# Reordering the first up-projections, and the scores and masks of chunk 1, in a fused attention and feed-forward kernel

## The chip, the cores and the metric

The kernel runs on one NeuronCore of a Trainium2 chip. The metric is device time in microseconds (us), the median of several executions; lower is better. Each comparison alternates runs of a kernel with runs of the kernel before on one chip.

## The reference

Sliding-window causal attention (8 batches, 8 heads, 576 positions, head size 64, window 64), then a feed-forward layer with a quick GELU over the 4608 tokens.

```python
scores = scale * np.matmul(q, k.transpose(0, 1, 3, 2))
mask = (rel >= 0) & (rel < window)            # rel = query position - key position
attn = softmax(np.where(mask, scores, -1e9))  # written out in the reference
attn_out = np.matmul(attn, v)
x = attn_out.transpose(0, 2, 1, 3).reshape(B * S, H * D)      # 4608 x 512
h = x @ w_in                                   # 512 -> 2048
g = h * (1.0 / (1.0 + np.exp(-1.702 * h)))
out = g @ w_out                                # 2048 -> 512
```

## The kernel before

Tokens are handled in 36 blocks of 128, attention by block (`scores`, `exp`, `mask`, `pv` for the value products, `norm`, then a transpose `x_mm` on TensorE and its copy `x_out`), the feed-forward by chunks of four blocks: 16 up-projections (`up`), each of a matmul part, a tanh on ScalarE and a gate on VectorE, then `down`. The program order is written by hand, and the trace shows an instruction that is ready wait for the one ahead of it: a mask whose exp had ended at 66.39 us started at 68.00, behind a gate. The matmuls write to tiles in PSUM from three pools: psH and psO with two buffers each, psT with one.

```python
def up_mm(ch, f, nf, t0, nt, wide=False):
    pool, tag = (psO, "O") if wide and next(turns) % 2 else (psH, "H")   # 2 buffers each
    ps = pool.tile([P, nf, nt], fp32, name="hps", tag=tag)
    ...                                   # nf x 4 matmuls
def up_th(ps, ...):  # ScalarE: th = tanh(0.851 * ps)
def up_g(th, ps, ...):  # VectorE: gT = (th + 1) * ps
def up(*args, **kw):
    up_g(*up_th(*up_mm(*args, **kw)))
```

The start: weights are loaded by GpSimd between its casts of values.

```python
for i in range(2):
    cast_v(0, i)
nc.gpsimd.tensor_copy(out=gate[0:1, 0:1], in_=stage_qk[1][0:1, 1, 0:1])
load_w_in(0)
cast_v(0, 2)
load_w_in(1)
cast_v(0, 3)
load_w_in(2)
load_w_in(3)
...
scores(3)
mask(2)
exp(3)
...
warm(6)                                   # six idle matmuls
pv(2)
norm(2)
u = up_mm(0, 0, 4, 0, P, wide=True)
mask(3)
x_mm(2, psO, "O")
x_out(2)
u = up_th(*u)
pv(3)
norm(3)
up_g(*u)
up(0, 0, 4, P, P, wide=True)
up(0, 0, 4, 2 * P, P, wide=True)
x_mm(3, psT, "T")
x_out(3)
up(0, 0, 4, 3 * P, P, wide=True)
for f in range(4, 16):
    up(0, f, 1, 0, 512, wide=True)
```

Chunk 1, in which attention of blocks 5 to 9 is woven between the up-projections of blocks 4 to 7:

```python
for m in range(4, 8):
    t0 = (m % 4) * P
    ...
    u = up_mm(1, 0, 4, t0, P, wide=True)
    pv(m + 1)
    up_g(*up_th(*u))
    norm(m + 1)
    up(1, 4, 4, t0, P, wide=True)
    ...                                   # m = 4, 6: turn_pairs, casts
    up(1, 8, 4, t0, P, wide=True)
    ...                                   # casts, loads, transposes for batch 2
    scores(m + 2)
    exp(m + 2)
    x_mm(m + 1, psT, "T")
    x_out(m + 1)
    up(1, 12, 4, t0, P, wide=True)
    mask(m + 2)
```

From chunk 2 on the order is by slots; from chunk 4 on x is transposed by DMA.

The softmax here doesn't subtract the row's maximum and nothing guards it: scores larger than these inputs give would overflow.

## Time and profile before

| | |
|---|---|
| timed at first | 323.79 us median of 3 (323.31 to 323.87) |
| profiled run | 328.4 us, span 326.7 us, mean clock 0.984 |
| TensorE busy | 94% of the span |
| VectorE, ScalarE, GpSimd busy | 51%, 48%, 42% |

The page's groups read: line, engine, operation, out<-in, shapes, count | busy us, mean ns of one | idle us of the engine just before them and what ended most of it. These two groups have the longest waits on VectorE and ScalarE:

```profile
L371 DVE SCALAR_TENSOR_TENSOR gT<-th,hps 128x512 bf16<-128x512 bf16 x144 | 99.0, 688 | 118.1 <-ACT th L365 118.0
L365 ACT ACTIVATE th<-hps 128x512 bf16<-128x512 f32 x144 | 86.1, 598 | 118.2 <-PE hps L354 109.3
```

The gates of VectorE wait for tanh, tanh waits for TensorE. Little of this idle time reached TensorE, which was busy for 94% of the span: it waited 3.2 us for masks (2.3 and 0.9 in the two groups of value products, L296). What cost time was an instruction queued behind such a waiting gate that could have run already and whose result TensorE wanted: for the mask at 68.00 us TensorE waited 0.78 us.

### The profile page before, as it was taken

What the parts mean: (1) busy time and instruction counts of PE and PEld (TensorE: products, weight loads), DVE (VectorE), ACT (ScalarE), POOL (GpSimd) and SP (SyncE); (2) the same over time, 40 slices, a digit from 0 to 9 for tenths busy, and PEclk for the clock granted to TensorE, in tenths of its full rate; (3) what the DMA queues carried; (4) which work ended last, traced back from release to release, by engine and by line L of the source; (5) the groups of instructions that cost most, each with busy time, mean ns of one, the idle gap of its engine ahead of it and who ended that gap; (6) DMA issues with size and microseconds to landing.
All of it is one profiled execution on the core that took longest, in us unless ns stands there. A gap on an engine that the chain in (4) does not pass through costs nothing.

```text
span 326.7 us, 7994 instructions
## 1 busy us (share of the span) xinstructions
PE 306.4 (94%) x3320; PEld 200.7 (61%) x3320; DVE 165.6 (51%) x284; ACT 157.5 (48%) x249; POOL 136.8 (42%) x197
## 2 busy tenths in 40 slices
PE   7888997777899899999999999999999999999995
PEld 7675453676777577777777777775555554444442
DVE  5666525556755536555556556555555554443300
ACT  2666416365555536545445455555545444344411
POOL 1880427856997677666776357700000000000000
PEclk9799999799999979999999999999999999999999
DMA  8999899999999999999999999934333311100021
GB/s 190 202 178 214 209 253 239 224 157 175 118 108 117 134 159 125 180 143 134 169 167 163 176 168 153 121 82 107 89 81 83 93 53 48 34 32 33 32 98 64
DMA packets 151524, 43.32 MB, mean 133 GB/s; under 512 B 135104, under 2 KB 146368, under 8 KB 151488
## 3 DMA queue, kind: packets, MB, share of 16 engines
q0 software_dynamic: 73008, 13.05, 60.1%
q1 hardware_dynamic: 74448, 22.43, 39.2%
q10 hardware_dynamic: 4032, 7.34, 6.5%
q8 instruction: 26, 0.43, 0.6%
q14 instruction: 10, 0.08, 0.1%
HBM read 36.70 MB, written 9.44 MB: 141 GB/s over the span
## 4 chain that ended last, share of the span: by engine, by line
PE 84%; DVE 5%; ACT 5%; DMA 3%; issue 1%; POOL 0%; POOLq 0%; ACTq 0%
PE ops L384 38%; PE hps L354 36%; PE Tacc L296 4%; PE S L267 3%; DMA kt<-rows_k 3%; ACT th L365 2%; PE idle L405 2%; DVE gT L371 1%; DVE PT L282 1%; ACT E L277 1%; PE turn L149 1%; ACT xT_pe L335 1%; PE pxt L330 1%; DVE qt L104 1%; DVE xs L309 1%
## 5 line engine op out<-in xcount | busy, mean ns | idle before, releaser
L371 DVE SCALAR_TENSOR_TENSOR gT<-th,hps 128x512 bf16<-128x512 bf16 x144 | 99.0, 688 | 118.1 <-ACT th L365 118.0
L384 PE MATMUL ops<-w_out_sb,gT 128*128 128x512 bf16 x576 | 144.4, 381 | 0.5 <-DVE gT L371 0.5
L365 ACT ACTIVATE th<-hps 128x512 bf16<-128x512 f32 x144 | 86.1, 598 | 118.2 <-PE hps L354 109.3
L354 PEld LDWEIGHTS <-w_in_sb 128*128 128x128 bf16 x1328 | 108.2, 114 | 43.8 <-issue 4.7
L384 PEld LDWEIGHTS <-gT 128*128 128x128 bf16 x576 | 53.2, 98 | 52.2 <-issue 1.1
L354 PE MATMUL hps<-xT_dma,w_in_sb 128*128 128x256 bf16 (+1 forms) x448 | 82.5, 318 | 0.0
L354 PE MATMUL hps<-xT_pe,w_in_sb 128*128 128x128 bf16 (+1 forms) x880 | 67.1, 232 | 3.5 <-ACT xT_pe L335 3.5
L277 ACT ACTIVATE E<-S 128x1024 bf16<-128x1024 f32 x36 | 36.7, 1020 | 3.6 <-PE S L267 3.6
L188 POOL DMA_DIRECT2D v_nat<-in_v_dram x25 | 21.3, 852 | 21.4 <-issue 12.4
L398 ACT ACTIVATE o_sb<-ops 128x512 f32<-128x512 f32 x34 | 20.4, 600 | 19.0 <-PE ops L384 18.7
L309 DVE TENSOR_TENSOR xs<-Tacc,rc 128x512 bf16<-128x512 f32 x36 | 24.9, 692 | 1.2
L282 DVE TENSOR_TENSOR PT<-E,mask_None 128x1024 bf16<-128x1024 bf16 x28 | 20.6, 737 | 1.7 <-ACT E L277 1.7
L192 POOL COPY v_off<-v_nat 64x528 bf16<-64x528 bf16 x25 | 15.6, 630 | 13.8 <-DMA v_nat<-in_v_dram 13.0
L187 POOL DMA_DIRECT2D rows_k<-in_k_dram x25 | 21.4, 854 | 0.0
L187 POOL DMA_DIRECT2D rows_q<-in_q_dram x25 | 21.1, 846 | 0.0
L267 PE MATMUL S<-qt,kt 64*128 64x64 bf16 x576 | 16.1, 191 | 5.0 <-DMA kt<-rows_k 1.6
L267 PEld LDWEIGHTS <-kt 64*128 64x128 bf16 x576 | 11.1, 95 | 12.9 <-issue 6.2
L296 PE MATMUL Tacc<-v_off,PT 128*64 128x65 bf16 x320 | 16.4, 200 | 0.9 <-DVE PT L282 0.9
L92 POOL CAST v_off<-stage_v 64x512 bf16<-64x512 f32 x15 | 9.4, 630 | 17.5 <-DMA stage_v<-in_v_dram 16.6
L296 PE MATMUL Tacc<-v_nat,PT 128*64 128x65 bf16 x256 | 14.6, 200 | 2.3 <-DVE PT L282 2.3
L296 PEld LDWEIGHTS <-PT 128*64 128x64 bf16 x576 | 12.4, 112 | 6.4 <-DVE PT L282 4.2
L194 POOL COPY v_off<-v_nat 64x528 bf16<-64x528 bf16 x20 | 13.2, 659 | 1.2
(47 smaller groups left out, 127.7 us busy)
## 6 DMA issues: line engine op xcount, KB each, us to landing
out_dram<-o_sb ACTq DMA_DIRECT2D x28, 256.0 KB, 3.2
stage_v<-in_v_dram SPq DMA_DIRECT2D x12, 256.0 KB, 6.5
rows_q<-in_q_dram POOLq DMA_DIRECT2D x20, 128.0 KB, 5.5
rows_k<-in_k_dram POOLq DMA_DIRECT2D x20, 128.0 KB, 5.9
v_nat<-in_v_dram POOLq DMA_DIRECT2D x20, 128.0 KB, 5.7
stage_qk<-in_q_dram SPq DMA_DIRECT2D x4, 512.0 KB, 5.4
stage_qk<-in_k_dram SPq DMA_DIRECT2D x4, 512.0 KB, 6.0
w_in_sb<-in_moe_w_in_dram POOLq DMA_DIRECT2D x4, 512.0 KB, 5.9
```

The costliest lines, as they stand in the source:

```text
L187: nc.gpsimd.dma_start(out=heads(rows[b % 2][w][0:n, i, :]), in_=rows_of(src, b, i))
L188: nc.gpsimd.dma_start(out=v_nat[b % 2][0:n, i, :, 0:D], in_=rows_of(v, b, i))
L267: nc.tensor.matmul(st[:, h % 2, t * 256 + hp * 64 : t * 256 + hp * 64 + 64], lhsT=src[1][part, hp, 64 * j : 64 * j + 128], rhs=src[0][part ...
L277: nc.scalar.activation(out=E_of[m][:], in_=S_of.pop(m)[:], func=AF.Exp, scale=scale)
L282: nc.vector.tensor_tensor(out=pt[:].rearrange("p a f -> p (a f)"), in0=E_of.pop(m)[:].rearrange("p a f -> p (a f)"), in1=masks[z][:].rearr ...
L296: nc.tensor.matmul(acc[t * 64 : t * 64 + 64, h // 4, (h % 4) * 66 : (h % 4) * 66 + 65], lhsT=pt[:, epos : epos + 64], rhs=win, start=True, ...
L309: nc.vector.tensor_tensor(out=xs[:].rearrange("p (b h d) -> p b h d", b=2, h=4), in0=view[:, :, :, 0:D], in1=rc[:].to_broadcast([P, 2, 4, D]),
L354: nc.tensor.matmul(ps[:, g, :], lhsT=w_in[:, c, (f + g) % 4 : 512 : 4], rhs=xT[ch][:, m0 : m0 + nt // P, c, :], start=(c == 0), stop=(c == 3),
L365: nc.scalar.activation(out=th[:], in_=ps[:], func=AF.Tanh, scale=0.851)
L371: nc.vector.scalar_tensor_tensor(out=gT[ch, f // 4][:, f % 4 : f % 4 + nf, t0 : t0 + nt], in0=th[:], scalar=1.0, in1=ps[:], op0=ALU.add, o ...
L384: nc.tensor.matmul(O_of[ch, tsub][:, :], lhsT=gT[ch, j][:, f, tsub * P : (tsub + 1) * P], rhs=w_out_sb[:, 4 * j + f, :], start=(j == 0 and ...
L398: nc.scalar.activation(out=o_sb[:], in_=ps[:], func=AF.Copy, scale=0.5)
```

## The change

Its intent: in chunk 0, to give TensorE up-projections to do while it waits for masks, normalising and x copies; in chunk 1, to run each mask while VectorE idles for the last tanh, and in blocks 5 and 7 to let exp start earlier by moving the scores up by one unit.

```diff
-    warm(6)
+    warm(4)
+    u0 = up_mm(0, 0, 4, 0, P, wide=True)
     pv(2)
     norm(2)
-    u = up_mm(0, 0, 4, 0, P, wide=True)
+    u1 = up_mm(0, 0, 4, P, P, wide=True)
+    u0 = up_th(*u0)
     mask(3)
     x_mm(2, psO, "O")
+    u1 = up_th(*u1)
     x_out(2)
-    u = up_th(*u)
+    up_g(*u0)
     pv(3)
     norm(3)
-    up_g(*u)
-    up(0, 0, 4, P, P, wide=True)
+    up_g(*u1)
     up(0, 0, 4, 2 * P, P, wide=True)
+    up(0, 4, 4, 0, P, wide=True)
     x_mm(3, psT, "T")
     x_out(3)
+    up(0, 4, 4, P, P, wide=True)
+    up(0, 4, 4, 2 * P, P, wide=True)
     up(0, 0, 4, 3 * P, P, wide=True)
-    for f in range(4, 16):
+    up(0, 4, 4, 3 * P, P, wide=True)
+    for f in range(8, 16):
         up(0, f, 1, 0, 512, wide=True)
...
     (chunk 1; the moved turn_pairs and casts are cut)
-        up(1, 8, 4, t0, P, wide=True)
...
+        if m in (4, 6):
+            up(1, 8, 4, t0, P, wide=True)
         scores(m + 2)
         exp(m + 2)
+        if m in (5, 7):
+            u = up_mm(1, 8, 4, t0, P, wide=True)
+            mask(m + 2)
+            up_g(*up_th(*u))
         x_mm(m + 1, psT, "T")
         x_out(m + 1)
-        up(1, 12, 4, t0, P, wide=True)
-        mask(m + 2)
+        u = up_mm(1, 12, 4, t0, P, wide=True)
+        if m in (4, 6):
+            mask(m + 2)
+        up_g(*up_th(*u))
```

More of the change, by code (lines that the diff above doesn't have):

```diff
@@ L536 @@
         up(1, 4, 4, t0, P, wide=True)
+        if m in (4, 6):
+            turn_pairs(1, m // 2 - 1, turn_tiles(psT, "T"))
         if m == 4:
-            turn_pairs(1, 1, turn_tiles(psT, "T"))
             cast_v(1, 2)
@@ L543 @@
             cast_v(1, 4)
-        if m == 6:
-            turn_pairs(1, 2, turn_tiles(psT, "T"))
-        up(1, 8, 4, t0, P, wide=True)
-        if m > 4:
+        else:
             cast_qk(2, m - 5)
@@ L555 @@
         load_v(2, m - 3)
+        if m in (4, 6):
+            up(1, 8, 4, t0, P, wide=True)
         scores(m + 2)
         exp(m + 2)
+        if m in (5, 7):
+            u = up_mm(1, 8, 4, t0, P, wide=True)
+            mask(m + 2)
+            up_g(*up_th(*u))
         x_mm(m + 1, psT, "T")
         x_out(m + 1)
-        up(1, 12, 4, t0, P, wide=True)
-        mask(m + 2)
+        u = up_mm(1, 12, 4, t0, P, wide=True)
+        if m in (4, 6):
+            mask(m + 2)
+        up_g(*up_th(*u))
     pe = {}
```

## The prediction

> **What bounds the kernel now.** I read the page first (busy shares, slices, chain), then the waits between engines, then each engine's timeline in 16 to 40 us (chunk 0) and 56 to 122 us (chunk 1 and the start of chunk 2), then DMA landings. Page of the kernel before:
>
> ```profile
> span 326.7 us, 7994 instructions
> PE 306.4 (94%) x3320; PEld 200.7 (61%) x3320; DVE 165.6 (51%) x284; ACT 157.5 (48%) x249; POOL 136.8 (42%) x197
> ...
> PE   7888997777899899999999999999999999999995
> ...
> PEclk9799999799999979999999999999999999999999
> ```
>
> TensorE is the bound: no other engine is over 51%, and from slice 16 on (8.17 us each) it is full. Only its gaps in slices 0 to 14 can be won. The clock row has three dips (slices 1, 7, 14). In 0.1 us windows, the clock is half from 12.99 to 16.37, 57.35 to 60.77 and 115.37 to 118.79 us. After about 125 us the waits view has no TensorE wait worth naming, so time won earlier should reach the end.
>
> The gaps of chunk 1, TensorE timeline (start, duration, operation, idle before and its releaser):
>
> ```profile
> 66.92 1.05 PE L354 MATMUL hps<-xT_pe,w_in_sb 128*128 128x128 bf16 x16 [0.44 <-ACT xT_pe L335]
> 68.75 0.22 PE L296 MATMUL Tacc<-v_nat,PT 128*64 128x65 bf16 x1 [0.78 <-DVE PT L282]
> ...
> 69.12 1.98 PE L354 MATMUL hps<-xT_pe,w_in_sb 128*128 128x128 bf16 x32
> 71.03 0.41 PE L267 MATMUL S<-qt,kt 64*128 64x64 bf16 x16
> 71.38 0.40 PE L330 MATMUL pxt<-ident,xs 128*128 128x128 bf16 x4
> 71.61 1.06 PE L354 MATMUL hps<-xT_pe,w_in_sb 128*128 128x128 bf16 x16
> 73.18 1.05 PE L354 MATMUL hps<-xT_pe,w_in_sb 128*128 128x128 bf16 x16 [0.52 <-ACT xT_pe L335]
> ```
>
> One block (up-projection 0, value products, up-projections 4 and 8, scores, x transposes, up-projection 12) takes 73.18 - 66.92 = 6.26 us, twice waiting: value products for a mask, the next block's first up-projection for the x copy. Why these come late, ScalarE and VectorE timelines:
>
> ```profile
> 65.36 1.03 ACT L277 ACTIVATE E<-S 128x1024 bf16<-128x1024 f32 x1
> 66.28 0.59 ACT L335 COPY xT_pe<-pxt 128x512 bf16<-128x512 bf16 x1
> 66.75 0.62 ACT L365 ACTIVATE th<-hps 128x512 bf16<-128x512 f32 x1
> ```
>
> ```profile
> 67.40 0.69 DVE L371 SCALAR_TENSOR_TENSOR gT<-th,hps 128x512 bf16<-128x512 bf16 x1 [1.21 <-ACT th L365]
> 68.00 0.68 DVE L282 TENSOR_TENSOR PT<-E,mask_None 128x1024 bf16<-128x1024 bf16 x1
> ```
>
> The exp ended at 66.39, yet its mask starts at 68.00, behind a gate that waited 1.21 us for a tanh. The x copy stands behind the exp, which starts only after the scores.
>
> [...] each dip is 3.4 us[...]. [...] the last dip follows one wait of 1.62 us. [...] In the trace, key transposes landed in 2.4 us (issued 65.98) to 8.2 us (issued 105.98), the latter beside GpSimd's loads[...].
>
> **The change, part by part.** Durations: an up-projection of 16 128x128 matmuls is 0.89 us on the chain, of four 128x512 0.865; its tanh starts 1.15 us after its start, tanh 0.60, gate 0.69, exp 1.02, mask 0.68, x copy 0.58, value products 0.38, scores 0.34, x transposes 0.24; normalising ends 1.48 after the value products start (68.75 to 70.23). Queued ScalarE and VectorE work starts some 0.09 us before its predecessor ends.
>
> *Chunk 0.* It removes two warm matmuls, fills the mask wait with real work, and splits four 512-wide up-projections into four 128-wide ones: 8x0.89 + 8x0.865 for 4x0.89 + 12x0.865, +0.1 us. Before, scores end at 18.93 and the last up-projection at about 36.6; the removable gaps there are 0.28, 0.20 and 0.94 plus two warms. After, step by step: the first up-projection waits for its weights (issued 13.54, landing 5.9 later, 19.44): 19.5 to 20.39. Value products 2 to 20.77, second up-projection to 21.66, x transposes 2 wait for normalising, 21.94. Mask 3 follows it on VectorE, to 22.46; value products 3 at 22.52 to 22.9. The x copy queues behind the second tanh, to 23.0; third up-projection 23.06 to 23.95. The fourth needs the PSUM buffer of the second, two psO allocations back, whose gate now queues behind normalising 3, to 24.6: 24.65 to 25.54, a **new wait** of 0.7. Then all is ready: x transposes 0.24, four 128-wide, eight 512-wide: 25.54 + 0.24 + 3.56 + 6.92 = 36.26. **Gain 0.35 us**, of 1.6 that one might hope for.
>
> *Chunk 1, masks ahead of gates.* The mask moves from 68.00 to 66.42, while VectorE idles for the gate's tanh. Value products start right after the up-projection, at 67.8 instead of 68.75: 0.95 for that block.
>
> *Chunk 1, scores one unit up* (blocks 5 and 7). Value products 67.81 to 68.19, up-projection 4 to 69.08, scores to 69.42; exp behind tanh 4, 69.8 to 70.82; up-projection 8 to 70.31; x transposes to 70.53, up-projection 12 to 71.42. Tanh 8 is 70.72 to 71.32, x copy 71.21 to 71.80: next block at 71.86, for 73.18. That is 4.94 us a block for 6.26, **1.32 each, 2.64 for two**, mask gain included. TensorE work alone is 4.45, so some 0.45 stays idle before each next block.
>
> *Block 6* (73.18 to 80.90, 7.72 us). Value products gain again, but transposes of pairs need the psT buffer that normalising frees, and normalising sits behind the first gate: they start 3.37 after the block's start, for 3.43 before. The rest gains where key copies no longer find VectorE behind a late gate: the next block at 78.92, 7.06 us, **gain 0.66**. Block 4 gains nothing before its end.
>
> Sum: 0.35 + 2.64 + 0.66 = **3.65 us**; chunk 2 starts at 83.5 instead of 87.16.
>
> *What lies after.* TensorE runs dense to 112.4, where scores of block 13 wait for keys:
>
> ```profile
> 114.27 0.29 PE L267 MATMUL S<-qt,kt 64*128 64x64 bf16 x8 [1.62 <-DMA kt<-rows_k]
> 114.87 1.44 PE L384 MATMUL ops<-w_out_sb,gT 128*128 128x512 bf16 x4
> ```
>
> Their transpose is issued behind an output store that follows TensorE, so both come 3.65 earlier and the lead stays. What changes is the neighbours: GpSimd's loads run ahead by their own clock. The issue moves to 102.3; the windows view shows a DMA share of 0.60 in 102 to 106, for 2.03 in 106 to 112.4. The wait may shrink, and with it the dip (estimate 1.8: pieces of 1.37, 1.71, 0.43 and 1.09 us on the chain for 0.86, 0.89, 0.22 and 0.86). Together up to 3.4 more.
>
> **Rivals.** (1) *The key wait goes too:* 3.65 + 3.4 = 7.05, 316.7 us. For it: the quieter DMA stretch. Against: loads issued from 103.35 still overlap, and the profiled run took 328.4 us for 323.79 unprofiled, so part of that wait may exist only under the profiler. (2) *The gain runs into DMA:* TensorE is 3.65 us nearer to its data and the same wait lengthens, leaving 1.5 to 2 us of gain, 322. For it: the view of waits has GpSimd waiting 8.0 us for loads in 60 to 125. Against: keys of batch 2 were issued by 83 with 3 to 6 us to land, long before use. (3) *ScalarE takes over in chunk 1*, delaying the x copies: gain under 2, 322. Against: 3.4 us of work in a block of 4.94. (4) [...] each dip is worth about 1.8 us either way; moving 0.35 us should keep the one at 57.
>
> **Range and chances.** The middle: 323.79 - 3.65 = 320.1; a third of rival 1's extra 3.4, less 0.2 for slips, gives 319.2. Low 316.6 is rival 1; high 321.6 is 2.2 us of gain, rival 2 or 3 in part. Over 2% needs 317.3, which asks for most of rival 1: 0.18. Slower by 2% would need several new waits: 0.01.
>
> **What would show it.** Right: no mask wait before value products of blocks 6 and 8; two blocks of about 4.9 us; a psO wait of about 0.7 before the fourth up-projection of chunk 0, whose end moves only some 0.35; chunk 2 beginning about 83.5. Wrong: blocks still over 5.5 us, an x copy later than ScalarE's order says, a longer key wait near 109 us, or another count of dips.

## The result

The changed kernel took 321.99 us (median of 4, 321.62 to 322.43), the kernel before 323.56 us (median of 4) beside it: ratio 0.9951, 95% interval 0.9934 to 0.9969. A ratio here is the mean time of one kernel's fast runs over that of the other's of the same rounds, so it is not quite the ratio of the medians. The gain was 1.6 us where the prediction's middle asked for 4.6, and the time lies 0.4 us above the stated range. All outputs are right.

The experiments repeated the comparison three times, the second and third on one chip, the fourth on another; the chip of the first is not on record:

| comparison | changed, median us | before, median us | ratio, 95% interval |
|---|---|---|---|
| first | 321.99 (4 runs) | 323.56 (4) | 0.9951, 0.9934 to 0.9969 |
| second | 321.19 (6) | 324.15 (11) | 0.9900, 0.9864 to 0.9936 |
| third | 321.51 (6) | 324.28 (12) | 0.9928, 0.9886 to 0.9969 |
| fourth | 321.65 (6) | 325.15 (11) | 0.9896, 0.9867 to 0.9924 |

The second and third share eleven runs of the kernel before, so they are not independent. The changed kernel's medians stayed within 321.2 to 322.0 us. The kernel before was lowest in the first comparison, the one the prediction is held against. By the later three the gain is 2.6 to 3.3 us (differences of means); all four are gains of under 2%.

Page of the changed kernel, first profile (clock in tenths of full speed, 40 slices):

```profile
span 320.7 us, 8047 instructions
...
PE   7869997798999999999999999999999999999994
...
PEclk9999999879999999999999999999999999999999
```

The spans of the two first profiles differ by 6.0 us, nearly four times the timed gain, and the trace says what the 6.0 is made of. The first down-projection began at 35.33 for 36.59 (1.26): the kernel before had half clock from 12.99 to 16.37 in its profile (granted clock 0.50; such a stretch of half clock is called a dip here), the changed one had not. Chunk 1 took 28.89 for 30.19 us (1.30), with two dips for one. From the start of chunk 2 to the end it took 236.1 for 239.5 (3.4): the wait for keys and the dip behind it were gone. So 4.7 of the 6.0 lie in dips and a wait that later profiles show to come and go. In chunk 1 it is the other way round: without dips the changed kernel takes 26.63 us there (runs 2, 4 and 5), so two dips, at 55.8 and at 66.0, hid 2.3 us of the gain in this execution, which is one of the four that were timed.

Block 7 of chunk 1 in the changed kernel, at full clock. TensorE's timeline (start, duration, what, count, idle before and releaser), then VectorE's:

```profile
79.57 1.05 PE L354 MATMUL hps<-xT_pe,w_in_sb 128*128 128x128 bf16 x16 [0.44 <-ACT xT_pe L335]
...
80.93 1.08 PE L354 MATMUL hps<-xT_pe,w_in_sb 128*128 128x128 bf16 x16
81.94 0.41 PE L267 MATMUL S<-qt,kt 64*128 64x64 bf16 x16
82.28 1.08 PE L354 MATMUL hps<-xT_pe,w_in_sb 128*128 128x128 bf16 x16
83.20 0.39 PE L330 MATMUL pxt<-ident,xs 128*128 128x128 bf16 x4
83.43 2.21 PE L354 MATMUL hps<-xT_pe,w_in_sb 128*128 128x128 bf16 x32
```

```profile
79.07 0.78 DVE L282 TENSOR_TENSOR PT<-E,mask_None 128x1024 bf16<-128x1024 bf16 x1 [0.23 <-ACT E L277]
80.05 0.69 DVE L371 SCALAR_TENSOR_TENSOR gT<-th,hps 128x512 bf16<-128x512 bf16 x1 [0.20 <-ACT th L365]
```

The mask now runs ahead of the gate, and the value products (the lines left out after the first) no longer wait. The last line holds two units, the second of chunk 2: it starts 2.21 - 1.05 = 1.16 us after 83.43, at 84.59. The block took 84.59 - 79.57 = 5.02 us, for 6.26 before; 4.94 was predicted.

Chunk 0 is another picture:

```profile
19.20 1.09 PE L354 MATMUL hps<-xT_pe,w_in_sb 128*128 128x128 bf16 x16 [1.65 <-DMA w_in_sb<-in_moe_w_in_dram]
20.59 1.08 PE L354 MATMUL hps<-xT_pe,w_in_sb 128*128 128x128 bf16 x16
...
22.84 1.95 PE L354 MATMUL hps<-xT_pe,w_in_sb 128*128 128x128 bf16 x32
...
35.33 1.03 PE L384 MATMUL ops<-w_out_sb,gT 128*128 128x512 bf16 x3
```

The first up-projection waited 1.65 us for its weights, with the value products of block 2 behind it. The third and fourth are one group of 1.95 us, twice 0.89 and a tail of some 0.16, so the fourth began at 22.84 + 0.89 = 23.73: the psO wait of 0.7 us that was predicted ahead of it is not there. VectorE's timeline has the gate of the second unit, for which it was to wait:

```profile
23.68 0.68 DVE L371 SCALAR_TENSOR_TENSOR gT<-th,hps 128x512 bf16<-128x512 bf16 x1
```

The gate was as late as predicted (it ended at 24.36, for 24.6), and the fourth up-projection started while that gate was still reading its tile. So the two did not share a buffer.

### The profile page after: what moved, and what is told of

It reads as the page before. It is cut to its first block, busy times and chain, and to the rows that moved or that the text cites. A ratio compares the mean times of both kernels' runs of the same rounds, so it can differ in the third digit from the quotient of the medians.

```text
span 320.7 us, 8047 instructions
## 1 busy us (share of the span) xinstructions
PE 299.2 (93%) x3329; PEld 200.6 (63%) x3366; DVE 164.7 (51%) x284; ACT 157.4 (49%) x249; POOL 135.3 (42%) x197
## 4 chain that ended last, share of the span: by engine, by line
PE 83%; ACT 5%; DMA 4%; DVE 3%; issue 3%; SPq 2%; POOL 0%; ACTq 0%
PE ops L384 38%; PE hps L354 37%; PE Tacc L296 4%; PE S L267 3%; DMA stage_qk<-in_k_dram 2%; DMA w_in_sb<-in_moe_w_in_dram 2%; ACT th L365 2%; ACT E L277 1%; ACT xT_pe L335 1%; PE turn L149 1%; DVE gT L371 1%; SPq L85 1%; SPq L119 1%; PE pxt L330 1%; DVE xs L309 1%
## 5 line engine op out<-in xcount | busy, mean ns | idle before, releaser
L384 PE MATMUL ops<-w_out_sb,gT 128*128 128x512 bf16 x539 | 136.6, 379 | 5.3 <-issue 4.1
L354 PEld LDWEIGHTS <-w_in_sb 128*128 128x128 bf16 x1376 | 110.5, 115 | 42.0 <-issue 2.3
L354 PE MATMUL hps<-xT_pe,w_in_sb 128*128 128x128 bf16 (+1 forms) x928 | 68.2, 230 | 3.5 <-DMA w_in_sb<-in_moe_w_in_dram 1.6
```

What stands on the lines that cost most here:

```text
L354: nc.tensor.matmul(ps[:, g, :], lhsT=w_in[:, c, (f + g) % 4 : 512 : 4], rhs=xT[ch][:, m0 : m0 + nt // P, c, :], start=(c == 0), stop=(c == 3),
L384: nc.tensor.matmul(O_of[ch, tsub][:, :], lhsT=gT[ch, j][:, f, tsub * P : (tsub + 1) * P], rhs=w_out_sb[:, 4 * j + f, :], start=(j == 0 and ...
```

## Experiments

My theory after the result: (A) chunk 1 gains as predicted; chunk 0 is paced by the landing of the first weights, so its reorder gives nothing; and the profile of the kernel before was a slow draw. Rivals: (B) the wait for keys is a standing cost that the change takes away; (C) chunk 0's new order costs time and eats part of chunk 1's gain; (D) half-clock dips eat it; later (E) the gain runs into a new wait on DMA. The runs came in four groups: runs 1 to 4, 5 to 8 and 9 to 12 on one chip, 13 to 15 on another. Each group is compared with runs of the kernel before; those of the second group are the first group's eleven and one more.

**1. The kernel before, unchanged.** No edit.

> The kernel before, unchanged, for a second profile. Theory A (the profile on record was a slow draw: it took 328.4 us where timed runs took 323.3 to 323.9): the new profile is near 322 us of span, has no 1.6 us wait for keys at scores of block 13, and at most two half-clock dips (mean clock 0.989 or more). Rival B (the key wait is in every run and the change removed it): the wait of 1 us or more shows again. Ratio to the kernel before 1.000 either way.

Measured: 324.97 us, ratio 1.0014 (0.9978 to 1.0049); profiled run 325.69 us, span 323.9 where theory A had 322.

```profile
18.92 1.08 PE L354 MATMUL hps<-xT_pe,w_in_sb 128*128 128x128 bf16 x16 [0.71 <-DMA w_in_sb<-in_moe_w_in_dram]
...
113.17 0.29 PE L267 MATMUL S<-qt,kt 64*128 64x64 bf16 x8 [1.48 <-DMA kt<-rows_k]
```

Theory A is half right. There was one dip and not three, and the weights already hold up the old order, by 0.71 us after its value products. But the wait for keys is there: part of rival B holds. In the five profiles without the whole new chunk 1 it was 1.62 (first), 1.48, 0.82 (run 3), 0.8 (run 9, masks alone) and none (run 10, scores alone).

**2. The changed kernel, unchanged.** No edit.

> The changed kernel, unchanged, as the control for the two halves. Both theories: ratio 0.993 to 0.997, about 1.6 us under the kernel before. Its profile should again show blocks of about 4.95 us where the clock is full.

Measured: 321.19 us, ratio 0.9900 (0.9864 to 0.9936), a larger gain than at first and than expected; no wait for keys. In this profile the weights held chunk 0 up twice:

```profile
18.93 1.08 PE L354 MATMUL hps<-xT_pe,w_in_sb 128*128 128x128 bf16 x16 [1.19 <-DMA w_in_sb<-in_moe_w_in_dram]
...
25.33 1.08 PE L354 MATMUL hps<-xT_pe,w_in_sb 128*128 128x128 bf16 x16 [1.71 <-DMA w_in_sb<-in_moe_w_in_dram]
...
36.95 1.03 PE L384 MATMUL ops<-w_out_sb,gT 128*128 128x512 bf16 x3
```

The second wait is for the second quarter of the weights, which the new order uses one unit earlier and ahead of the x transposes of block 3. That load landed 8.2 us after its issue here and 5.5 in the first profile.

**3. Chunk 0 alone.** The first hunk of the diff on the kernel before.

> Only the reordering of chunk 0. Theory A (chunk 0 is paced by the landing of the first weights at about 19.2 us, and the new order does not shorten what follows): ratio 0.999 to 1.002. Prediction on record: 0.35 us, ratio 0.9989. Rival C (the new order of chunk 0 costs time, and eats part of chunk 1's gain): ratio 1.002 to 1.005, 0.6 to 1.6 us slower.

Measured: 324.64 us, ratio 1.0014 (0.9984 to 1.0044). The reorder of chunk 0 shows no gain; one of 0.35 us (0.9989) lies inside the interval, one of 0.6 does not. Its first up-projection began at 19.38 and the first down-projection at 35.50.

**4. Chunk 1 alone.** The second hunk on the kernel before.

> Only the reordering of chunk 1. Prediction on record: 3.3 us, ratio 0.990. Theory A (a half-clock dip that moves into or stays in chunk 1 hides part of it): ratio 0.993 to 0.996. Rival C (chunk 0's reorder loses what chunk 1 wins): ratio 0.988 to 0.991 here, clearly under the whole change.

Measured: 321.14 us, ratio 0.9903 (0.9872 to 0.9933), 3.2 us by the means. That is the whole of the change's gain on this chip. Between the first up-projection of block 4 and that of chunk 2 the profile has 26.63 us (55.85 to 82.48) for 29.90 in run 3 (55.87 to 85.77), neither with a dip there: 3.27 us, where 2.64 + 0.66 = 3.30 had been worked out. Run 3, then run 4, whose last line again holds two units, the second of chunk 2 (81.32 + 1.16):

```profile
55.87 1.05 PE L354 MATMUL hps<-xT_pe,w_in_sb 128*128 128x128 bf16 x16 [0.67 <-ACT xT_pe L335]
...
85.77 1.05 PE L354 MATMUL hps<-xT_pe,w_in_sb 128*128 128x128 bf16 x16 [0.52 <-ACT xT_pe L335]
```

```profile
55.85 1.05 PE L354 MATMUL hps<-xT_pe,w_in_sb 128*128 128x128 bf16 x16 [0.67 <-ACT xT_pe L335]
...
81.32 2.21 PE L354 MATMUL hps<-xT_pe,w_in_sb 128*128 128x128 bf16 x32
```

**5. The changed kernel again.** No edit.

> The changed kernel once more, to pool with the two earlier comparisons (0.9951 and 0.990): ratio 0.989 to 0.996. Theory A: the wait for the first weights shows again (0.5 to 1.7 us before the first up-projection), and no wait for a psO buffer before the fourth up-projection. Prediction on record: a psO wait of about 0.7 us there.

Measured: 321.51 us, ratio 0.9928 (0.9886 to 0.9969). The wait for the first weights was 0.96 us, no psO wait, chunk 1 again 26.63 us. A new wait shows in chunk 4, the first chunk whose x is transposed by DMA:

```profile
149.37 1.06 PE L354 MATMUL hps<-xT_dma,w_in_sb 128*128 128x256 bf16 x8 [0.95 <-DMA xT_dma<-xs]
```

That transpose was issued at 141.10 and landed 8.2 us later. No profile with the old chunk 1 has such a wait, nor has that of run 9; with the whole new chunk 1 it was 0.35 in run 4, 0.95 here, 0.47 in run 7 and 1.45 in run 8, and none on the matmuls in runs 2, 6 and 15 and in the first profile. This is theory E: some of the gain is handed to DMA in some executions. The wait for keys is gone in all of these profiles but run 7's, which has one of 1.13 us.

**6. The changed kernel with earlier weights.**

```diff
-    for i in range(2):
-        cast_v(0, i)
+    cast_v(0, 0)
+    load_w_in(0)
+    cast_v(0, 1)
     nc.gpsimd.tensor_copy(out=gate[0:1, 0:1], in_=stage_qk[1][0:1, 1, 0:1])
-    load_w_in(0)
-    cast_v(0, 2)
     load_w_in(1)
-    cast_v(0, 3)
+    cast_v(0, 2)
     load_w_in(2)
+    cast_v(0, 3)
     load_w_in(3)
```

> The changed kernel with each weight load of w_in issued one cast earlier on GpSimd, so that the first is issued near 10 instead of 13 us. Theory A (chunk 0 is paced by the landing of the weights): the wait at the first up-projection goes, chunk 0 ends 1 to 2 us earlier, ratio to the kernel before 0.983 to 0.990. Rival (the reorder of chunk 0 is worthless for another reason, for example a wait for x copies): the wait for weights goes but chunk 0 ends within 0.4 us of 35.3 us and the ratio stays at 0.989 to 0.996.

Measured: 319.99 us, ratio 0.9874 (0.9842 to 0.9905).

```profile
18.54 1.83 PE L354 MATMUL hps<-xT_pe,w_in_sb 128*128 128x128 bf16 x16 [0.90 <-DMA w_in_sb<-in_moe_w_in_dram]
```

The load was issued at 9.97 for 13.0 to 13.4 us, yet the matmuls began at 18.54, only some 0.5 earlier: it took 8.5 us to land, for 5.7 to 6.1. Why it took longer was not shown. The expectation that the wait would go was wrong. The duration of 1.83 for 1.08 is a dip (18.7 to 22.1) that followed the wait. The median is 1.5 us under run 5's, but the intervals overlap.

**7. Earlier weights, old order in chunk 0, new chunk 1.** The edit of run 6 on the kernel of run 4.

> Old order in chunk 0, new order in chunk 1, weight loads issued earlier as in the run above. Theory A: with the weights early, the old order of chunk 0 has its 0.94 us wait for an x copy and its waits for masks again, and ends 0.7 to 1.3 us later than the new order does with early weights. Rival: both orders end chunk 0 within 0.3 us of each other.

Measured: 321.01 us, ratio 0.9897 (0.9864 to 0.9931). From the first up-projection to the first down-projection the old order took 34.66 - 18.49 = 16.17 us. The new order takes 16.13 wherever neither dip nor second wait disturbs it (first profile, runs 3 and 5). The rival holds for the time after the landing (chunk 0 of run 6 itself ended later, at 36.16, with its dip): once the weights have landed both orders are equally long. The old one has its 0.94 us wait for an x copy; the new one has the value products of block 2 to do after the landing, which the old one does before it.

**8. The two gaps ahead of block 4 filled with idle matmuls.**

```diff
     down_out(0, 3, on_dve=True)
+    warm(18)
     x_mm(4, psT, "T")
+    warm(10)
     x_out(4)
```

> The changed kernel with 28 idle matmuls put into the two gaps of 1.06 and 0.67 us ahead of block 4[...]. Theory D (half-clock dips near 56 us cost part of the gain in some executions): no dip between 50 and 62 us, mean clock 0.995 or more in all runs, and a median 0.4 to 1.0 us under the plain changed kernel. Rival (dips are paid in another place anyway, or cost nothing because TensorE waits for others there): within 0.3 us of the plain changed kernel.

Measured: 322.34 us, ratio 0.9941 (0.9899 to 0.9983), mean clock 0.989 to 0.995: no better than the plain change, so the remedy of theory D fails. Stretches of 5 us (length, busy time of PE, PEld, DVE, ACT and POOL with counts, then granted clock, DMA share, GB/s), of the changed kernel's first profile and of this run:

```profile
55.00:60.00 5.00, 3.97 (x49) 3.51 (x47) 3.12 (x6) 1.96 (x4) 4.69 (x7) 0.66 0.99 298
...
65.00:70.00 5.00, 4.56 (x71) 4.11 (x70) 3.07 (x6) 2.07 (x5) 3.35 (x6) 0.66 1.02 202
```

```profile
55.00:60.00 5.00, 4.54 (x86) 4.02 (x80) 3.96 (x7) 2.72 (x5) 4.69 (x7) 1.00 0.75 242
...
65.00:70.00 5.00, 4.56 (x63) 4.20 (x64) 2.82 (x5) 2.70 (x5) 4.58 (x7) 0.66 1.30 156
```

The dip at 55 to 60 is gone, and the one at 65 to 70 stands, behind the waits for key copies of block 6 (1.01 and 0.38 us) that nothing filled. Another came at 18.7, after the wait of 1.12 us for weights.

**9. Masks alone.** On the kernel before:

```diff
-        up(1, 12, 4, t0, P, wide=True)
+        u = up_mm(1, 12, 4, t0, P, wide=True)
         mask(m + 2)
+        up_g(*up_th(*u))
```

> The kernel before with one edit: in each block of chunk 1 the mask is put ahead of the last gate; the scores stay where they were, and chunk 0 too. By the recurrence of the prediction a block of chunk 1 then takes 5.3 us instead of 6.26 (value products at once, the next x copy behind tanh 8 and exp): chunk 1 gains 2 x 0.9 + 0.7 = 2.5 us. Ratio 0.990 to 0.995. Rival (the scores carry the gain): block over 5.9 us, gain under 1 us.

Measured: 321.71 us, ratio 0.9916 (0.9873 to 0.9959), 2.8 us by the means. TensorE's timeline in chunk 1:

```profile
65.22 1.05 PE L354 MATMUL hps<-xT_pe,w_in_sb 128*128 128x128 bf16 x16 [0.44 <-ACT xT_pe L335]
...
70.63 1.05 PE L354 MATMUL hps<-xT_pe,w_in_sb 128*128 128x128 bf16 x16 [0.52 <-ACT xT_pe L335]
```

Block 5 took 70.63 - 65.22 = 5.41 us and chunk 1 27.42 (55.77 to 83.19), 2.48 under run 3; 2.5 had been expected. The masks carry three quarters of the gain in the traces, by one moved line that runs four times.

**10. Scores alone.** The kernel of run 4 with each mask behind the last gate again.

> The kernel before with the scores of blocks 5 and 7 moved up by one unit, the masks still behind the last gate. By the same recurrence a block takes 5.8 us instead of 6.26 and the wait of 0.8 us for the mask stays: gain 2 x 0.45 = 0.9 us, ratio 0.996 to 0.999. Rival: as large as the masks alone, 2 us or more.

Measured: 323.38 us, ratio 0.9986 (0.9938 to 1.0033), which by itself is no clear gain. Chunk 1 took 29.14 (55.80 to 84.94), 0.76 under run 3, for 0.9 expected, and the mask wait stays:

```profile
67.22 0.22 PE L296 MATMUL Tacc<-v_nat,PT 128*64 128x65 bf16 x1 [0.93 <-DVE PT L282]
```

In the traces the two moves add up: 2.48 + 0.76 = 3.24, for 3.27 together.

**11. The changed kernel with x transposes one slot earlier.**

```diff
-            later(s + 2, lambda m=m: x_dma(m))
+            later(s + 1, lambda m=m: x_dma(m))
```

> The changed kernel with each transpose of x by DMA put one slot earlier in program order, right behind its normalising. Theory E (the gain runs into DMA: TensorE arrives at chunk 4 before the x transpose has landed, a wait of 0.3 to 1.4 us seen in the profiles with the new chunk 1 and in none with the old one): that wait is under 0.2 us, and the median 0.3 to 1 us under the changed kernel's. Rival (the transpose is issued earlier but lands no earlier because the DMA engines are full): the wait stays over 0.3 us.

Measured: 325.27 us, ratio 1.0017 (0.9976 to 1.0059): a miss. The wait for x is gone, and all of the change's gain with it. Three waits for keys appear, the longest this one:

```profile
167.45 0.29 PE L267 MATMUL S<-qt,kt 64*128 64x64 bf16 x8 [1.76 <-DMA kt<-rows_k]
```

They make 3.3 us in all, in chunks 4 and 5, where run 5 has none. The x transposes are issued on the sync queue with those of queries and keys (SPq L338 and L199 in the trace), and in the new program order stand ahead of more of them. That the waits for keys come from this order was not shown.

**12. A combination:** new chunk 1, the earlier weights of run 6, the x transposes of run 11, and in chunk 0 the old order with one later unit as filler:

```diff
     x_mm(3, psT, "T")
     x_out(3)
+    up(0, 4, 4, 0, P, wide=True)
     up(0, 0, 4, 3 * P, P, wide=True)
-    for f in range(4, 16):
+    up(0, 4, 4, P, P, wide=True)
+    up(0, 4, 4, 2 * P, P, wide=True)
+    up(0, 4, 4, 3 * P, P, wide=True)
+    for f in range(8, 16):
         up(0, f, 1, 0, 512, wide=True)
```

> A version built from what the runs showed: new chunk 1; weight loads one cast earlier; x transposes one slot earlier; in chunk 0 the value products of block 2 stay ahead of the first up-projection (they fit into the wait for weights), and one 128-wide up-projection of the second weights fills the 0.94 us wait for the x copy of block 3. Theory A: first up-projection to the end of chunk 0 takes 15.2 to 15.5 us instead of 16.1, ratio to the kernel before 0.980 to 0.987, under every run so far. Rival: ratio 0.987 to 0.990, no better than early weights with the new order.

Measured: 324.15 us, ratio 0.9997 (0.9948 to 1.0046). Chunk 0 did what was expected, 34.00 - 18.64 = 15.36 us, but waits for keys took 5.5 us. With run 11 this points at the x transposes.

The last three runs asked for the cause of chunk 0's failed term.

**13. The hybrid:** run 12's chunk 0 and the new chunk 1, weight loads and x transposes as in the kernel before.

> New chunk 1; chunk 0 with value products of block 2 ahead of the first up-projection as before, and one 128-wide unit of the second weights as filler of the 0.94 us wait; weight loads as in the kernel before. Theory A: first up-projection to end of chunk 0 in 15.3 us (16.1 with the whole change) when the second weights land by 23 us, up to 1.5 us more when they land at 25; ratio to the kernel before 0.985 to 0.991, at or below the whole change. Rival (the end of chunk 0 does not carry to the end of the kernel): chunk 0 shorter, ratio as the whole change.

Measured: 319.38 us, ratio 0.9848 (0.9804 to 0.9892).

```profile
18.86 1.08 PE L354 MATMUL hps<-xT_pe,w_in_sb 128*128 128x128 bf16 x16 [0.67 <-DMA w_in_sb<-in_moe_w_in_dram]
...
20.48 1.98 PE L354 MATMUL hps<-xT_pe,w_in_sb 128*128 128x128 bf16 x32
...
22.52 11.74 PE L354 MATMUL hps<-xT_pe,w_in_sb 128*128 128x128 bf16 x112
34.09 1.03 PE L384 MATMUL ops<-w_out_sb,gT 128*128 128x512 bf16 x4
```

34.09 - 18.86 = 15.23 us: the value products fit into the wait for weights, the filler takes the x-copy wait, and the rest is one dense group. On this chip its mean is 4.9 us under that of the kernel before. Its mean is also 1.5 under the changed kernel's, and five of its six runs lie under all six of run 15, but the sixth took 323.40 and the intervals overlap: likely faster than the changed kernel, not shown.

**14. The hybrid with earlier weights.** Run 13 with the edit of run 6.

> As the run above with the weight loads one cast earlier: chunk 0 ends near 34.0 us as it did in the combined version, and no wait for keys of 3 us or more, since the x transposes are back in their old slots. Theory A: ratio 0.982 to 0.988, the fastest of all. Rival (a TensorE that is a further 1 to 2 us ahead finds keys or x transposes not landed): ratio 0.987 or more, with a wait on DMA of over 1.5 us in its profile.

Measured: 319.83 us, ratio 0.9855 (0.9805 to 0.9905). Chunk 0 ended at 34.84, not near 34.0, and the profile has a wait for x of 0.4 us and none for keys. No gain of the earlier loads over the hybrid is seen; no wait of 1.5 us shows either, so the rival's mechanism is not borne out.

**15. The changed kernel once more,** beside runs 13 and 14.

> The whole change once more for the pool: ratio 0.989 to 0.996. Wait for the first weights of 0.9 us or more, then 16.1 us to the end of chunk 0 unless the second weights land late.

Measured: 321.65 us, ratio 0.9896 (0.9867 to 0.9924). The wait for the first weights was 1.22 us, then 16.13 us to the end of chunk 0, as expected. Its profile has two dips in chunk 1 again, at 55.5 and 65.7, and chunk 1 took 28.92 us, 2.3 more than in runs 2, 4 and 5: so the first profile was no single accident. The ratio of the six runs is as good as run 2's all the same.

## Why the prediction was right or wrong

The middle of 4.6 us was 3.3 for chunk 1, 0.35 for chunk 0 and 1.1 for the wait for keys, less 0.2 for slips.

**What bounds the kernel: right.** Time won in chunk 1 reached the end: 3.27 us in the trace, 3.2 in the timed runs of run 4.

**Chunk 1: right where no dip falls into it.** Masks ahead of gates and scores one unit up came out singly (runs 9 and 10) and together (run 4): 3.27 us for 3.3. That the sum fits to the hundredth is luck: blocks 5 and 7 gained 1.25 each for 1.32, and block 6 took 7.14 us, 0.78 under run 3 but 0.58 under the first profile's 7.72, for 0.66. (TensorE's work in a block adds up to 4.50 us by the prediction's own steps, not 4.45.) Both mask waits disappeared as described. ScalarE as the new bound (rival 3) did not come.

**Chunk 0: wrong.** The step that failed is "Gain 0.35 us", in two ways. It counted a psO wait of 0.7 us before the fourth up-projection. No profile has it, and the trace shows that the gate which was to free the buffer was still at work when the fourth began. I had assumed that the two buffers are dealt out by turns, and here they were not: the fourth started at 23.73 us, while the gate ran from 23.68 to 24.36. Which tile it took instead was not shown. And it took the start from a profile in which half clock had delayed the scores to 18.93, so that the weights at 19.44 looked almost no obstacle. Run 3's profile had such a dip too (13.1 to 16.5), and its chunk 0 ended at 35.50 for 36.59, 1.09 us earlier: the 0.35 and the 0.7 that did not come. In the other profiles the last scores end between 17.2 and 18.0, the first weights arrive between 18.4 and 19.3, and the new order makes the value products wait with the up-projection (0.90 to 1.65 us). From there both orders take 16.1 to 16.2 us where no dip and no late second weights disturb them, and run 3's timing shows no gain. Chunk 0 ended at 35.08 to 35.33 with the new order (first profile, runs 5 and 15), at 35.42 and 35.48 with the old one (runs 10 and 4), so some 0.2 us may remain, and in run 2 late second weights (issued at 17.10 us and 8.2 us in landing, for 17.06 and 5.5 in the first profile) took more than that. Run 13, which leaves the value products in front, takes 15.2: the idea of filling the waits was sound, the place of the value products was not.

**The credit for the key wait: mis-sized.** "A third of rival 1's extra 3.4" put 1.1 us into the middle and stood behind the range's low end of 316.6. In the profile pair the 3.4 is there in full, but the first profile was one slow execution, as the prediction had itself suspected from 328.4 against 323.79. The runs showed in its place a key wait of 0 to 1.6 us with the old order, mostly gone with the new one, and given back in part as a wait of up to 1.45 us for the x transposes of chunk 4 (runs 4, 5, 7, 8). That is rival 2's mechanism at a place that the prediction did not look at: it followed keys, not x. In the timed runs no credit is seen: run 4 gained 3.2 us, chunk 1's share alone. How much of rival 1 is real stays open.

**The range: too narrow at the top.** 2.2 us of gain was its upper end. With nothing from chunk 0 and nothing from the key wait, 3.3 us of chunk 1 less some dips and x waits gives 2 to 3 us, and the first comparison measured 1.6.

**Dips: mis-sized, and one more came.** Rival 4 put each at 1.8 us and expected the one at 57 to stay: the first was estimated from the pieces of the dip at 115, the ground of the second was not shown. The profile of the scored comparison has that one (55.8) and a second at 66.0, and they cost 2.3 us of chunk 1's 3.3; it has no wait for keys or on the matmuls for x, so in this execution the dips are the loss that the trace shows. (The kernel before pays for dips too, but less there: 0.3 us of its chunk 1 in the first profile and in run 1.) By block, the dip near 56 cost 0.3 to 0.8 us (block 4 took 9.71 to 10.26 us for 9.45), the one near 66 1.4 to 1.5 (block 5 6.40 to 6.51 for 5.01: first profile, runs 8 and 15). The one at 115 in the kernel before did cost its 1.8: from chunk 2 on 239.5 us, less the wait of 1.62, for 236.1 in run 10. Over the 33 runs of the kernel before in the later groups, time rises with the loss of mean clock by 152 us per 1.00 (correlation 0.54); a dip of 3.4 us at half clock lowers the mean clock by 0.0053, which makes 0.8 us a dip. This is an association, not an experiment; run 8 failed to remove the dips. What sets one off was not shown: the one at 66.0 us began after separate gaps of 1.01, 0.39 and 0.44 us, with TensorE busy for 1.77 of the 3.4 us before, and run 2's profile has gaps of 1.01, 0.39 and 0.43 us at the same places and no dip in chunk 1.

**What stays open:** why the first comparison shows 1.6 us and the later ones 2.6 to 3.3. The intervals of the first and the second overlap only just, the changed kernel's medians agree within 0.8 us, and it is the kernel before that was lower in the first. Dips can be part of it: two of the four changed runs had the mean clock of 0.989 that goes with two dips. But run 15 had three of six such executions and a full gain, and the clocks of the kernel before are not on record for the first comparison. No run tells chance from chip here.

## What to carry to other kernels

Put an instruction whose inputs are ready ahead of one that is known to wait for another engine, where the trace shows the first held up by the second, as the mask at 68.00 us was here: four moved masks gave 2.48 of chunk 1's 3.27 us. Before moving work forward, ask what it waits for and what then stands behind it: in run 13 the value products, which could start at once, stood in front of the load that had not landed and a later up-projection in the gap after it, and chunk 0 took 15.23 us from its first up-projection for 16.13. A schedule worked out from one profile inherits that profile's luck (two profiles of the kernel before had spans of 326.7 and 323.9 us, with mean clocks of 0.984 and 0.993), so take a second one before sizing a step by a single wait.
